# First token tiles as half-depth transposes, weights on ScalarE's queue, and partial accumulation groups at the start of a two-branch attention kernel

## The chip, the cores and the metric

The kernel runs on one core of a Trainium2 chip. The metric is device time in microseconds of that core: the median of the fast runs. A profile of one execution is there for every kernel. "Start of the K projection" below is the start of the first matmul of the second stage in such a trace; it measures the first stage, the only one that the change touches. In the profiles PE is TensorE (PEld its weight loads), DVE VectorE, ACT ScalarE, POOL GpSimd and SP the sync engine; the granted clock is the share of TensorE's full clock that the throttle let through.

## The reference

```python
def reference(A_x, A_wqkv, A_wo, B_x, B_wqkv, B_wo, gate_w):   # x: 1 x 2048 x 1024, bf16
    x = A_x
    g = sigmoid((x * gate_w).sum(-1, keepdims=True))
    a = linear_attention(x, A_wqkv, A_wo)        # 32 heads of 32, phi = elu + 1
    b = dilated_local_attention(x, B_wqkv, B_wo) # window 8, dilation 2, softmax
    return g * a + (1 - g) * b
```

The kernel first computes branch B's values, V = x @ wqkv[:, 2048:3072], for 16 token tiles of 128, in two halves of 512 columns each; then K and Q, attention and the rest.

## The kernel before

`xT` holds x transposed: 8 blocks of 128 model dimensions ("depth") on the partitions, tokens along the free axis. A DMA transpose fills it, one token tile per instruction. `ws[0]` holds the 1024 value columns as two halves; half 0 comes in four pieces of two depth blocks (256 KB each). SP is the engine that issues most DMAs, and it does so in order; the rest of its stream is stores of V.

```python
def load_x(t, prio):                      # a full tile: 128 tokens x 1024, 256 KB
    e_, r = t // 8, t % 8
    P.op("sp", lambda e: e.dma_start_transpose(xT[:, :, t*128:(t+1)*128], x2[e_, r*128:(r+1)*128, :]), ...)
def load_w(slot, half, src, c0, prio, d0=0, d1=8, eng="sp", after=()):
    P.op(eng, lambda e: e.dma_start(ws[slot][:, d0:d1, half*512:half*512+512], src[:, d0:d1, c0:c0+512]), ...)

load_x(0, 0)
load_w(0, 0, Bw, 2048, 0.1, 0, 2, "act")
load_w(0, 0, Bw, 2048, 0.2, 2, 4, "act")
load_w(0, 0, Bw, 2048, 0.3, 4, 6)
load_w(0, 0, Bw, 2048, 0.4, 6, 8)
for t in range(1, NT): load_x(t, 3 + t)
for d in range(0, 8, 2): load_w(0, 1, Bw, 2560, 6.1 + 0.1 * d, d, d + 2)   # second weight half
# ... 9 warm-up matmuls on a zero tile go ahead of everything on PE ...
for t, half in [(4*b + i, half) for b in range(NT // 4) for half in range(2) for i in range(4)]:
    # ...
    step = 2 if t == 0 else 8
    for d in range(0, 8, step):
        o = group(bank, xs, w, [xr, ws[0].part((d, d + step), ...)], d, d + step)   # 8 matmuls 128x128x512
    move(vt[:, :], bank.ap, 512, bank, vt.all())       # eviction on ScalarE or VectorE
    P.op("sp", ... store of vt to HBM ..., prio=5)
```

A planner orders each engine's instructions from estimated costs and priorities (a low number goes first). A changed cost or priority can therefore also reorder stages that the edit does not touch.

## Time and profile before

495.04 us (three runs, 494.76 to 495.15).

The page of the kernel before: its span, the busy time of each engine, and the group of V-type matmuls (count, busy time, mean ns, idle time ahead of them).

```profile
span 493.6 us, 11394 instructions
...
PE 477.7 (97%) x5055; PEld 226.2 (46%) x5121; DVE 274.7 (56%) x487; ACT 166.9 (34%) x287; POOL 5.1 (1%) x27
...
L1313 PE MATMUL ps_all<-w,xT 128*128 128x512 bf16 x921 | 207.5, 380 | 5.4 <-issue 4.3
...
```

TensorE is busy for 97% of the span. There are 5121 weight loads but only 5055 matmuls, and 921 in a group that has 960 in the changed kernel's page. So 66 matmul records are missing, and where one is, the trace seems to show a gap. I fell for this in the prediction: the "gaps of about 0.16 us per attention fill", and the "stall" of 0.22 us at 15.4 us, are missing records. The latter recurs after every 49 records (at 26.19 us again, the starts 0.431 us apart, two matmuls' time), and traces with all records have neither.

Stretches of 5 us of the kernel before: busy time (number of instructions) for each engine, granted clock, mean busy share of the DMA engines (the packets' times over that of 16 engines, so it can exceed 1), and what they moved.

```profile
...
core 0: us, PE busy (x) PEld busy (x) DVE busy (x) ACT busy (x) POOL busy (x), PEclk, DMA share, GB/s
...
5.00:10.00 5.00, 4.63 (x19) 1.74 (x19) 0.43 (x2) 0.64 (x2) 0.61 (x3) 1.00 1.10 253
10.00:15.00 5.00, 4.93 (x24) 2.05 (x23) 0.69 (x1) 1.15 (x2) 0.00 (x0) 1.00 1.07 263
15.00:20.00 5.00, 4.95 (x24) 2.29 (x24) 0.69 (x1) 1.19 (x2) 0.00 (x0) 1.00 0.87 208
...
```

The DMA issues of SP in the first 11 us of the kernel before: start, duration, what, count.

```profile
...
0.80 1.37 SPq L1287 DMA_TRANSPOSE xT<-in_A_x_dram  x1
2.23 1.07 SPq L1292 DMA_DIRECT2D w<-in_B_wqkv_dram  x2
3.35 4.82 SPq L1287 DMA_TRANSPOSE xT<-in_A_x_dram  x3
8.21 2.13 SPq L1292 DMA_DIRECT2D w<-in_B_wqkv_dram  x4
...
```

Reading: a full transpose occupies SP for about 1.3 us (one of the three at 3.35 us took 2.18, presumably with the queue full) and a plain weight piece for about 0.5. The second weight half goes out at 8.2 us, when four tiles are on their way.

The waits of PE and of its weight loads (PEld) from 5 to 30 us, before: who waited for what, total us, times, longest.

```profile
...
PEld ps_all L1313 <- DMA xT<-in_A_x_dram: 1.8, 2, 1.3
...
PEld ps_all L1313 <- DMA w<-in_B_wqkv_dram: 0.8, 2, 0.6
...
PE ps_all L1313 <- DMA xT<-in_A_x_dram: 0.4, 1, 0.4
```

One short wait for the first tile, one for the second at 8.0 us, one for the second weight half at 14.7 us.

### The profile page before, as it was taken

What the parts mean: (1) busy time and instruction counts of PE and PEld (TensorE: products, weight loads), DVE (VectorE), ACT (ScalarE), POOL (GpSimd) and SP (SyncE); (2) the same over time, 40 slices, a digit from 0 to 9 for tenths busy, and PEclk for the clock granted to TensorE, in tenths of its full rate; (3) what the DMA queues carried; (4) which work ended last, traced back from release to release, by engine and by line L of the source; (5) the groups of instructions that cost most, each with busy time, mean ns of one, the idle gap of its engine ahead of it and who ended that gap; (6) DMA issues with size and microseconds to landing.
All of it is one profiled execution on the core that took longest, in us unless ns stands there. A gap on an engine that the chain in (4) does not pass through costs nothing.

```text
span 493.6 us, 11394 instructions
## 1 busy us (share of the span) xinstructions
PE 477.7 (97%) x5055; PEld 226.2 (46%) x5121; DVE 274.7 (56%) x487; ACT 166.9 (34%) x287; POOL 5.1 (1%) x27
## 2 busy tenths in 40 slices
PE   8999999999999999999999999999999999999995
PEld 3444444444444445545554544444444444444442
DVE  2112345899676785564555555596865735524443
ACT  2111111222334345656565465455432223020000
POOL 3000000000000000000000000000000000000000
PEclk9999999999999999999999999999999999999999
DMA  8989992222003155111010100503564325101122
GB/s 225 212 206 322 307 371 62 86 86 85 14 23 110 29 161 141 28 36 35 24 35 25 35 3 3 171 1 80 124 182 117 76 38 153 65 1 66 65 85 68
DMA packets 51067, 48.80 MB, mean 99 GB/s; under 512 B 20161, under 2 KB 38977, under 8 KB 51010
## 3 DMA queue, kind: packets, MB, share of 16 engines
q1 hardware_dynamic: 50466, 47.47, 34.5%
q8 instruction: 42, 0.69, 0.6%
q10 hardware_dynamic: 544, 0.52, 0.3%
q14 instruction: 15, 0.12, 0.1%
HBM read 34.34 MB, written 9.44 MB: 89 GB/s over the span
## 4 chain that ended last, share of the span: by engine, by line
PE 89%; DMA 3%; SPq 3%; issue 2%; DVE 2%; ACT 1%; ACTq 0%
PE ps_all L1313 71%; PE ps_all L1634 11%; PE ps_all L1405 2%; PE ps_all L1424 2%; DMA rb<-rc_hbm 1%; SPq L1287 1%; PE ps_all L1506 1%; SPq L1598 1%; DMA w<-in_B_wqkv_dram 1%; PE ps_all L1431 1%; DMA rc_hbm<-ra 1%; DVE zsel L1548 1%; SPq L1292 1%; DVE pq L1326 0%; PE ps_all L1585 0%
## 5 line engine op out<-in xcount | busy, mean ns | idle before, releaser
L1313 PE MATMUL ps_all<-w,xT 128*128 128x512 bf16 x921 | 207.5, 380 | 5.4 <-issue 4.3
L1313 PE MATMUL ps_all<-xT,w 128*128 128x512 bf16 x748 | 167.5, 379 | 2.3 <-issue 1.7
L1313 PEld LDWEIGHTS ps_all<-w,xT 128*128 128x128 bf16 x960 | 91.3, 98 | 109.8 <-DMA xT<-in_A_x_dram 1.8
L1313 PEld LDWEIGHTS ps_all<-xT,w 128*128 128x128 bf16 x768 | 73.7, 98 | 89.1 <-issue 1.8
L1634 PE MATMUL ps_all<-w,qT 128*128 128x512 bf16 (+1 forms) x259 | 55.3, 373 | 0.3
L1634 PEld LDWEIGHTS ps_all<-w,qT 128*128 128x128 bf16 x264 | 25.8, 98 | 29.7
L1324 DVE TENSOR_SCALAR e<-e 128x512 bf16<-128x512 bf16 x64 | 18.3, 291 | 33.8 <-ACT e L1320 17.2
L1344 DVE CAST vst<-ps_all 128x512 bf16<-128x512 f32 x15 | 10.4, 692 | 44.0 <-PE ps_all L1313 44.0
L1411 ACT ACTIVATE E<-ps_all 128x1824 bf16<-128x1824 f32 (+1 forms) x18 | 30.4, 1687 | 9.8 <-PE ps_all L1405 9.0
L1322 ACT ACTIVATE e<-ps_all 128x512 bf16<-128x512 f32 x32 | 19.1, 597 | 42.8 <-PE ps_all L1313 42.8
L1414 DVE TENSOR_TENSOR E<-E,msk 128x1824 bf16<-128x1824 bf16 (+1 forms) x18 | 19.8, 1102 | 22.1 <-ACT E L1411 22.1
L1638 DVE SCALAR_TENSOR_TENSOR o<-ps_all,gm,xT 128x512 bf16<-128x512 f32 (+1 forms) x25 | 18.2, 730 | 23.0 <-PE ps_all L1634 22.8
L1320 ACT ACTIVATE e<-ps_all 128x512 bf16<-128x512 f32 x32 | 19.1, 597 | 26.8 <-PE ps_all L1313 25.8
L1345 ACT ACTIVATE vst<-ps_all 128x512 bf16<-128x512 f32 x17 | 10.1, 597 | 47.7 <-PE ps_all L1313 47.7
L1274 DVE TENSOR_TENSOR mx<-mx,kT 128x1024 bf16<-128x1024 bf16 x32 | 20.8, 688 | 9.3 <-ACT kT L1345 9.2
L1274 DVE TENSOR_TENSOR mx<-mx,qT 128x1024 bf16<-128x1024 bf16 x32 | 20.8, 687 | 6.9 <-ACT qT L1348 6.7
L1443 DVE TENSOR_TENSOR qT<-ps_all,L 128x456 bf16<-128x456 f32 (+1 forms) x36 | 21.0, 627 | 6.2 <-ACT L L1441 5.0
L1326 DVE SCALAR_TENSOR_TENSOR pk<-ps_all,e 128x512 bf16<-128x512 f32 x32 | 21.9, 688 | 0.7
L1440 ACT ACTIVATE L<-ps_all 128x456 f32<-128x456 f32 (+1 forms) x36 | 17.8, 547 | 12.4 <-PE ps_all L1424 12.4
L1345 ACT ACTIVATE kT<-ps_all 128x512 bf16<-128x512 f32 x16 | 9.6, 597 | 35.8 <-PE ps_all L1313 35.8
L1601 DVE TENSOR_TENSOR xT<-xT,rb 128x512 bf16<-128x512 bf16 x24 | 16.3, 689 | 8.7 <-DMA rb<-rc_hbm 8.5
L1348 ACT ACTIVATE qT<-ps_all 128x512 bf16<-128x512 f32 x16 | 9.6, 597 | 31.5 <-PE ps_all L1313 31.5
(72 smaller groups left out, 284.1 us busy)
## 6 DMA issues: line engine op xcount, KB each, us to landing
rb<-rc_hbm SPq DMA_DIRECT2D x32, 256.0 KB, 5.1
w<-in_A_wqkv_dram SPq DMA_DIRECT2D x6, 1024.0 KB, 8.5
v<-vB_hbm SPq DMA_DIRECT2D x36, 128.0 KB, 2.9
vB_hbm<-vst SPq DMA_DIRECT2D x32, 128.0 KB, 5.9
w<-in_B_wqkv_dram SPq DMA_DIRECT2D x4, 1024.0 KB, 9.0
xn<-in_A_x_dram SPq DMA_DIRECT2D x16, 256.0 KB, 2.7
out_dram<-o SPq DMA_DIRECT2D x15, 256.0 KB, 2.0
w<-in_A_wo_dram SPq DMA_DIRECT2D x8, 256.0 KB, 4.1
```

Source lines behind the costliest of these rows:

```text
L1274: P.op("dve", lambda e, m=m, op=op: e.tensor_tensor(m[:, 0:n], m[:, 0:n], src, op), 0.08 + n / 1920.0, reads=[m.all(), reg], writes=[m.all()],
L1313: last = e.matmul(bank.ap(), lhs(dc), rhs(dc), start=(dc == 0), stop=(dc == 7))
L1320: P.op("act", lambda e: e.activation(e_[:, :], bank.ap(), ACT.Exp), act(512), reads=[bank.iv], writes=[e_.all()])
L1322: P.op("act", lambda e: e.activation(e_[:, :], bank.ap(), ACT.Exp, accum_out=qe[:, col:col + 1]), act(512) + 0.1, reads=[bank.iv], writes= ...
L1324: P.op("dve", lambda e: e.tensor_scalar(e_[:, :], e_[:, :], 1.0, 1e-6, op0=ALU.min, op1=ALU.add), 0.25, reads=[e_.all()], writes=[e_.all()])
L1326: P.op("dve", lambda e: e.scalar_tensor_tensor(out=dst, in0=bank.ap(), scalar=0.0, in1=e_[:, :], op0=ALU.max, op1=ALU.add), dps(512), read ...
L1345: fa = lambda e: e.activation(dst, src(), ACT.Copy)
L1411: P.op("act", lambda e: e.activation(E[:, 0:32 * nq].rearrange("p (j q) -> p j q", j=4), ps[:, 4:8, 0:8 * nq], ACT.Exp), act(32 * nq), rea ...
L1414: P.op("dve", lambda e: e.tensor_tensor(ev(), ev(), m[:, :, :].rearrange("p r q -> p (r q)")[:, None, :].to_broadcast([128, 16, 2 * nq]), ...
L1443: P.op("dve", lambda e, L=L, h=h, q0=q0: e.tensor_tensor(qT[:, :, q0:q0 + nq], SO[h].ap(0, n).rearrange("p (c q) -> p c q", c=8), L[:, 0:n ...
L1634: last = e.matmul(bank.ap(0, f1 - f0), qT[:, dc, t * 128:(t + 1) * 128], ws[3][:, dc, f0:f1], start=(dc == 0), stop=(dc == 7))
L1638: P.op("dve", lambda e, bank=bank, o_=o_, t=t, n=n, i0=i0, i1=i1, tgt=tgt, c0=c0: e.scalar_tensor_tensor(out=o_[:, i0 * 128:i1 * 128].rear ...
```

## The change

The intent: let the first matmuls start on half of a tile's depth and half of the weights, take weight issues off SP, and delay the need for the second weight half by running eight token tiles, not four, on the first. The first pass does depth blocks 0 to 3 of tiles 0 to 3 into four PSUM banks, the second pass blocks 4 to 7.

```diff
-        load_x(0, 0)
-        load_w(0, 0, Bw, 2048, 0.1, 0, 2, "act")
-        load_w(0, 0, Bw, 2048, 0.2, 2, 4, "act")
-        load_w(0, 0, Bw, 2048, 0.3, 4, 6)
-        load_w(0, 0, Bw, 2048, 0.4, 6, 8)
-        for t in range(1, NT):
-            load_x(t, 3 + t)
         for d in range(0, 8, 2):
-            load_w(0, 1, Bw, 2560, 6.1 + 0.1 * d, d, d + 2)
+            load_w(0, 0, Bw, 2048, 0.1 + 0.1 * d, d, d + 2, "act")
+        for b in range(2):
+            for t in range(4):
+                P.op("sp", lambda e, t=t, b=b: e.dma_start_transpose(xT[:, 4 * b:4 * b + 4, t * 128:(t + 1) * 128], x2[0, t * 128:(t + 1) * 128, 512 * b:512 * b + 512]),
+                     0.8, writes=[xT.part((4 * b, 4 * b + 4), (t * 128, (t + 1) * 128))], prio=4 * b + t, chan="x%d_%d" % (t, b), lat=0.6)
+        for t in range(4, NT):
+            load_x(t, 8 + t)
...
-        for t, half in [(4 * b + i, half) for b in range(NT // 4) for half in range(2) for i in range(4)]:
+        for t, half in [(t, half) for t0, n in ((0, 8), (8, 4), (12, 4)) for half in range(2) for t in range(t0, t0 + n)]:
...
-            bank = main.next()
...
-            step = 2 if t == 0 else 8
-            for d in range(0, 8, step):
-                o = group(bank, xs, w, [xr, ws[0].part((d, d + step), (half * 512, half * 512 + 512))], d, d + step)
+            cuts = [0, 8]
+            if t < 4 and half == 0:
+                cuts = [0, 2, 4, 6, 8] if t == 0 else [0, 4, 8]
+                if t == 0:
+                    first = [main.next() for _ in range(4)]
+                    for t_ in range(4):
+                        for d, d1 in ((0, 2), (2, 4)) if t_ == 0 else ((0, 4),):
+                            group(first[t_], x_tile(t_)[0], w, [...], d, d1)
+                    o = P.ops[-1]
+                    for d in range(0, 8, 2):
+                        load_w(0, 1, Bw, 2560, 3 + 0.1 * d, d, d + 2, "act", after=[o])
+                cuts = cuts[len(cuts) // 2:]
+                bank = first[t]
+            else:
+                bank = main.next()
+            for d, d1 in zip(cuts, cuts[1:]):
+                o = group(bank, xs, w, [...], d, d1)
```

More of the change, by code (lines that the diff above doesn't have):

```diff
@@ L1356, in plan @@
                  (12, 1): (3, 0, Aw, 1024, 25), (14, 1): (3, 1, Aw, 1536, 26)}
-        for t, half in [(4 * b + i, half) for b in range(NT // 4) for half in range(2) for i in range(4)]:
+        for t, half in [(t, half) for t0, n in ((0, 8), (8, 4), (12, 4)) for half in range(2) for t in range(t0, t0 + n)]:
             vt, vs = vst.next()
             xs, xr = x_tile(t)
-            bank = main.next()
             w, wr = w_half(0, half)
-            step = 2 if t == 0 else 8
-            for d in range(0, 8, step):
-                o = group(bank, xs, w, [xr, ws[0].part((d, d + step), (half * 512, half * 512 + 512))], d, d + step)
+            cuts = [0, 8]
[5 more added lines that the diff above has]
+                        for d, d1 in ((0, 2), (2, 4)) if t_ == 0 else ((0, 4),):
+                            group(first[t_], x_tile(t_)[0], w, [xT.part((d, d1), (t_ * 128, t_ * 128 + 128)), ws[0].part((d, d1), (0, 512))], d, d1)
+                    o = P.ops[-1]
[6 more added lines that the diff above has]
+            for d, d1 in zip(cuts, cuts[1:]):
+                o = group(bank, xs, w, [xT.part((d, d1), (t * 128, t * 128 + 128)), ws[0].part((d, d1), (half * 512, half * 512 + 512))], d, d1)
             move(vt[:, :], bank.ap, 512, bank, vt.all())
```

## The prediction

> **What bounds the kernel.** TensorE. The page gives PE 477.7 us busy of 493.6 (97%), with the granted clock full in the 40 slices. Busy time by windows is 89.6 of 90 us from 20 to 110 us; later there are gaps of about 0.16 us per attention fill and one of 1 us near 370 us. Only start-up losses can be won.
>
> **Start-up losses, from the start times in the trace.** Nine warm-up matmuls run from 1.25 to 5.27 us. The first real matmul starts at 5.62, released by the first token tile (landed at 5.58). The first real matmuls start 0.40, 0.43 and 0.31 us apart, later ones 0.216: the clock rises at about 6.7 us. This agrees with the Trainium skill, "TensorE: Matmul & The Clock Gate", Part 1 (cold array at half rate, full after a few us of activity). Then come stalls: about 0.19 us at 8.0 (second token tile, landed 7.97), 0.24 at 14.7 and 0.22 at 15.4 us (second weight half; the waits view names the same DMAs). Sum: 0.35 late start, 0.48 slow clock, 0.64 stalls. The change does not move the clock, and the warm-ups stay ahead on PE: the first real matmul cannot start before 5.27. As those 0.35 us lie in the slow clock, starting earlier wins only half of them. So at most 0.18 + 0.64 = 0.8 us is to be had.
>
> **What it moves.** Matmuls, weight loads and evictions stay in number and shape. Four full transposes (about 1.3 us of SP issue each) become eight halves; I estimate 0.7 to 0.8 us each. ScalarE issues the four first-half weight pieces (0.45 us each) from 0.8 to 2.7 us, SP only transposes. The second weight half is issued by ScalarE after the first 16 matmuls instead of by SP at 8.2 us. Data need for PE: before, 3 MB (both weight halves, 4 tiles) for 64 matmuls; after, 3 MB too (one weight half, 8 tiles), but tile 4 is needed after 32.
>
> **Will data keep up?** DMA moves about 290 GB/s in this stage (windows). The Trainium skill, "DMA: Bandwidth & Descriptors", Queues, rings and completion order, says that each DMA engine round-robins between queues per packet; the trace agrees: from 4.0 to 4.5 us 143 packets of 256 B (transpose) beside 120 of 1024 B (ScalarE's queue). So weights get most bandwidth: 1 MB of weights by about 6.4 us, with the first halves of tiles 0 and 1 beside them. Estimated landings of half tiles: 4.2, 6.7 (needed 6.9), 7.4 (7.8), the others 8 to 10 (from 9.5). Tiles 4 to 7 about 11, 12, 15.5, 16.5 (needed 13, 14.6, 16.4, 18). Just in time; I expect a new stall of 0 to 0.4 us.
>
> **Prediction.** Gain 0.18 + 0.64 - 0.15 = about 0.65 us: 494.4 us, range 493.0 to 495.9. Faster by over 2%: 0.005, within 2%: 0.985, slower: 0.01.
>
> **Signs.** First real matmul at 5.3 us, not 5.6; no wait for weights at 14 to 16 us; half transposes of 0.65 to 0.85 us on SP; the 128th real matmul about 0.65 us earlier; slices from 20 us on unchanged, PE busy about 477. Wrong if: half transposes cost as much issue as full ones, so that tiles 4 to 7 come late and stalls appear at 12 to 18 us; ScalarE blocks on its DMA issues and evictions hold banks; or the re-made instruction order shifts a later stage (rb reads near 370 us, tail) by a microsecond.

## More of the kernel before

The transposes up to 30 us: count, min/median/max ns that they occupy SP, and time from issue to landing.

```profile
...
L1287 SPq DMA_TRANSPOSE xT<-in_A_x_dram x13: 1248/1308/2569, 0.8 to 28.9; - x13
...
DMA to landing us min/median/max: 3.2/4.1/5.3
```

## The result

| | median us | runs | ratio, 95% interval |
|---|---|---|---|
| before | 495.1 | 6 (494.76 to 496.3) | |
| changed | 501.99 | 6 (499.54 to 503.08) | 1.0130 (1.0105 to 1.0156) |

A ratio is the mean time of one kernel's fast runs over that of the other's of the same rounds, so it is not quite the ratio of the medians. The change made the kernel slower by 1.3%, where a gain of 0.13% had been forecast.

The page of the changed kernel, profiled in its fastest run (499.54 us), so it shows 4 of the 6.9 us between the medians:

```profile
span 497.7 us, 11467 instructions
...
PE 484.9 (97%) x5121; PEld 226.2 (45%) x5121; DVE 274.1 (55%) x484; ACT 168.7 (34%) x290; POOL 5.1 (1%) x27
...
L1312 PE MATMUL ps_all<-w,xT 128*128 128x512 bf16 x960 | 213.9, 379 | 5.9 <-DMA xT<-in_A_x_dram 5.9
...
```

The stretches of 5 us, as for the kernel before:

```profile
...
5.00:10.00 5.00, 2.52 (x11) 0.91 (x11) 0.43 (x2) 0.00 (x0) 0.62 (x3) 1.00 1.17 214
10.00:15.00 5.00, 5.00 (x24) 2.05 (x21) 2.08 (x3) 0.00 (x0) 0.00 (x0) 1.00 0.61 138
15.00:20.00 5.00, 1.90 (x9) 0.70 (x8) 0.69 (x1) 0.60 (x1) 0.00 (x0) 1.00 1.21 243
...
```

From 5 to 10 us PE is busy 2.52 us instead of 4.63, and from 15 to 20 us 1.90 instead of 4.95. From 10 to 15 us the DMA engines move 138 GB/s where they moved 263.

What PE did in the first 30 us of the changed kernel (start, length, what, count, idle time ahead and what ended it):

```profile
...
6.04 1.04 PE L1312 MATMUL ps_all<-w,xT 128*128 128x512 bf16 x4 [0.77 <-DMA xT<-in_A_x_dram]
8.79 6.22 PE L1312 MATMUL ps_all<-w,xT 128*128 128x512 bf16 x28 [1.70 <-DMA xT<-in_A_x_dram]
16.27 1.90 PE L1312 MATMUL ps_all<-w,xT 128*128 128x512 bf16 x8 [1.27 <-DMA xT<-in_A_x_dram]
20.30 9.89 PE L1312 MATMUL ps_all<-w,xT 128*128 128x512 bf16 x45 [2.13 <-DMA xT<-in_A_x_dram]
```

Four gaps, 5.87 us in all, each ended by a token tile. The waits of the same stretch agree, and no other wait has taken their place:

```profile
...
PEld ps_all L1312 <- DMA xT<-in_A_x_dram: 8.5, 5, 2.6
PE ps_all L1312 <- DMA xT<-in_A_x_dram: 5.9, 4, 2.1
...
```

SP's issues:

```profile
...
0.80 10.51 SPq L1299 DMA_TRANSPOSE xT<-in_A_x_dram  x8
11.35 9.17 SPq L1287 DMA_TRANSPOSE xT<-in_A_x_dram  x4
20.56 0.58 SPq L1378 DMA_DIRECT2D vB_hbm<-vst  x1
...
```

Eight halves occupy SP until 11.3 us. Tile 4 is issued at 11.35 us; before, all four tiles and both weight halves were out at 10.3. The transposes by line (the first line is the halves), and the landings up to 30 us:

```profile
...
L1299 SPq DMA_TRANSPOSE xT<-in_A_x_dram x8: 1245/1270/1330, 0.8 to 10.0; - x8
L1287 SPq DMA_TRANSPOSE xT<-in_A_x_dram x8: 1247/1310/3812, 11.3 to 29.4; - x8
...
DMA to landing us min/median/max: 2.7/4.4/7.8
```

The half transposes take 1.27 us of SP each, the full ones 1.31.

The budget from the two traces: the first real matmul starts 0.42 us later (6.04 against 5.62), the V stage from there to the K projection takes 60.88 us instead of 56.18, and the rest is 1.1 us shorter (425.12 against 426.23 us from the start of the K projection to PE's end). Together +4.0 us. The 1.1 us belong to no part of the change: e6_order below has before's instruction order on PE and 425.12 us too, and over all profiles of these kernels the rest takes 425.12 to 426.23 us. It is mostly one gap of 0.98 us at 370 us in the one trace of before. With a single trace of that kernel I can't tell how often it has it.

### The profile page after: what moved, and what is told of

Its sections match the earlier page's. It is cut to its first block, busy times and chain, and to the rows that moved or that the text cites. A ratio compares the mean times of both kernels' runs of the same rounds, so it can differ in the third digit from the quotient of the medians.

```text
span 497.7 us, 11467 instructions
## 1 busy us (share of the span) xinstructions
PE 484.9 (97%) x5121; PEld 226.2 (45%) x5121; DVE 274.1 (55%) x484; ACT 168.7 (34%) x290; POOL 5.1 (1%) x27
## 3 DMA queue, kind: packets, MB, share of 16 engines
HBM read 34.34 MB, written 9.44 MB: 88 GB/s over the span
## 4 chain that ended last, share of the span: by engine, by line
PE 93%; SPq 2%; DMA 2%; DVE 1%; issue 0%
PE ps_all L1312 76%; PE ps_all L1646 11%; PE ps_all L1417 2%; SPq L1299 2%; PE ps_all L1436 2%; DMA xT<-in_A_x_dram 2%; PE ps_all L1518 1%; PE ps_all L1443 1%; DVE zsel L1560 1%; PE ps_all L1597 0%; DVE pq L1325 0%; SPq L1287 0%; PE ps_all L1570 0%; DVE e L1323 0%; DVE w L1343 0%
## 5 line engine op out<-in xcount | busy, mean ns | idle before, releaser
L1312 PE MATMUL ps_all<-w,xT 128*128 128x512 bf16 x960 | 213.9, 379 | 5.9 <-DMA xT<-in_A_x_dram 5.9
L1312 PE MATMUL ps_all<-xT,w 128*128 128x512 bf16 x768 | 170.7, 379 | 0.0
L1426 DVE TENSOR_TENSOR E<-E,msk 128x1824 bf16<-128x1824 bf16 (+1 forms) x18 | 19.8, 1102 | 22.1 <-ACT E L1423 22.1
L1344 ACT ACTIVATE kT<-ps_all 128x512 bf16<-128x512 f32 x18 | 10.7, 597 | 34.7 <-PE ps_all L1312 34.7
L1325 DVE SCALAR_TENSOR_TENSOR pk<-ps_all,e 128x512 bf16<-128x512 f32 x32 | 21.9, 687 | 0.7
L1347 ACT ACTIVATE qT<-ps_all 128x512 bf16<-128x512 f32 x18 | 10.8, 597 | 31.1 <-PE ps_all L1312 31.1
```

Of the source, the lines that this page charges most:

```text
L1312: last = e.matmul(bank.ap(), lhs(dc), rhs(dc), start=(dc == 0), stop=(dc == 7))
L1325: P.op("dve", lambda e: e.scalar_tensor_tensor(out=dst, in0=bank.ap(), scalar=0.0, in1=e_[:, :], op0=ALU.max, op1=ALU.add), dps(512), read ...
L1344: fa = lambda e: e.activation(dst, src(), ACT.Copy)
L1426: P.op("dve", lambda e: e.tensor_tensor(ev(), ev(), m[:, :, :].rearrange("p r q -> p (r q)")[:, None, :].to_broadcast([128, 16, 2 * nq]), ...
```

## The experiments

Two theories. The **issue theory**: a DMA transpose occupies SP for about 1.27 us whatever its depth, so halving tiles 0 to 3 costs four extra instructions and halves the rate at which tokens arrive. The **share theory**: weight pieces on ScalarE's queue reach the DMA engines ahead of the transposes on SP's, which land late. Third suspects: the order of eight tiles, the partial groups, the second weight half on ScalarE's queue, and the clock.

All runs gave correct results; ratios are to the kernel before in the same rounds. "First" and "K" are the start of the first real matmul and of the K projection in the one profiled run.

| run | what | median us | ratio (95%) | first | K |
|---|---|---|---|---|---|
| before | | 494.9 to 495.7 | 1 | 5.62 | 61.80 |
| changed | | 501.99 | 1.0130 (1.0105 to 1.0156) | 6.04 | 66.93 |
| after_again | the same, again | 501.70 | 1.0123 (1.0109 to 1.0138) | 5.33 | 69.34 |
| e1_full | changed, halves undone | 502.21 | 1.0138 (1.0108 to 1.0168) | 6.14 | 67.77 |
| e2_w1late | changed, second weight half on SP | 500.81 | 1.0101 (1.0086 to 1.0115) | 5.94 | 70.90 |
| e3_w_back | changed, two first-half pieces back on SP | 501.35 | 1.0135 (1.0117 to 1.0153) | 5.46 | 67.83 |
| e4_halves_only | before, halves alone | 499.46 | 1.0091 (1.0078 to 1.0104) | 5.66 | 65.89 |
| e5_act_weights_only | before, two pieces to ScalarE alone | 497.20 | 1.0049 (1.0033 to 1.0066) | 6.13 | 63.27 |
| e6_order | before, order of eight alone | 495.91 | 1.0005 (0.9991 to 1.0019) | 5.70 | 63.16 |
| e9_partial_order | before, order and partial groups | 497.33 | 1.0043 (1.0026 to 1.0060) | 5.77 | 63.62 |
| e10_halves_order | before, order and halves | 500.65 | 1.0110 (1.0093 to 1.0127) | 5.62 | 67.39 |
| e8_fill | changed, stalls filled | 501.27 | 1.0127 (1.0112 to 1.0141) | 5.50 | 68.21 |
| e12_full_fill | e1_full, stall filled | 499.96 | 1.0080 (1.0061 to 1.0099) | 6.05 | 66.74 |
| e7_order_den | e6, denominators later | 495.51 | 0.9995 (0.9981 to 1.0009) | 5.80 | 63.32 |
| e11_order_w1soon | e6, second half sooner | 495.27 | 1.0000 (0.9987 to 1.0013) | 5.86 | 62.32 |

### e0_sizes: what a transpose costs SP

```diff
-        for t in range(1, NT): load_x(t, 3 + t)
+        for t in [1, 2, 3, 4, 5, 6, 7, 13, 15]: load_x(t, 3 + t)
+        # tile 8: 4 x (128 rows x 256 columns), tile 9: 8 x (128 x 128), tile 10: 2 x (64 x 1024),
+        # tile 11: 2 x (128 x 512), tile 12: 4 x (32 x 1024), tile 14: 8 x (16 x 1024)
```

> The kernel before, with tiles 8 to 12 and 14 loaded in pieces of several shapes, to measure what one transpose costs SP. Issue theory (a transpose costs SP's queue about 1.27 us whatever its depth): pieces of 512, 256 and 128 columns by 128 rows all take 1.2 to 1.3 us where nothing blocks the queue; pieces with fewer rows tell whether rows set it. Share theory (the 1.27 us of the halves is back-pressure of the DMA engines, busy with weights): pieces issued later, when little else moves, take about 0.65, 0.35 and 0.2 us for 512, 256 and 128 columns. The kernel as a whole will be slower than before (some 25 more transposes on SP), which is of no interest.

All transposes of that run, pieces first (min/median/max ns on SP):

```profile
...
L1302 SPq DMA_TRANSPOSE xT<-in_A_x_dram x28: 1099/1176/2131, 20.0 to 71.0; - x28
L1287 SPq DMA_TRANSPOSE xT<-in_A_x_dram x10: 1237/1310/2461, 0.8 to 72.3; - x10
...
```

By shape, from the start and length of each instruction in the trace, with the queue not blocked:

| rows x columns | KB | us on SP |
|---|---|---|
| 128 x 1024 | 256 | 1.24 to 1.38 |
| 128 x 512 | 128 | 1.27 |
| 64 x 1024 | 128 | 1.27 |
| 128 x 256 | 64 | 1.17 |
| 32 x 1024 | 64 | 1.18 |
| 128 x 128 | 32 | 1.10 to 1.23 |
| 16 x 1024 | 32 | 1.10 to 1.23 |

The cost is nearly all fixed: an eighth of the bytes takes 1.10 to 1.23 us where the whole takes 1.24 to 1.38, even at 30 to 70 us, far from the crowded start. Back-pressure is ruled out as the cause of the 1.27 us, and the issue theory's premise holds. It is the cost where nothing blocks; four transposes of this run, left out of the table, took 1.58 to 2.46 us. The whole run took 516.14 us, a single look.

### after_again: the changed kernel a second time

> The changed kernel unaltered, to have it on the same chip and a second profile. Expected: ratio to before 1.010 to 1.016, first real matmul near 6.0 us, stalls of about 1.7 us near 7, 1.3 near 15 and 2.1 near 18 us. Its runs should spread by 3 us, the slower ones with a lower mean granted clock (0.991 to 0.998); if the profile catches such a run it should show matmuls 0.427 us apart for some microseconds after one of the stalls.

Ratio and stalls as expected in kind, though of other sizes: 1.50 us ahead of tile 1, 3.15 ahead of tile 4, 0.66 ahead of tile 5. This profile (502.43 us) caught what the first did not. Its stretches from 10 to 25 us:

```profile
...
10.00:15.00 5.00, 4.60 (x22) 1.86 (x19) 2.08 (x3) 0.37 (x1) 0.00 (x0) 1.00 0.79 156
15.00:20.00 5.00, 2.25 (x6) 0.88 (x7) 0.00 (x0) 0.23 (x1) 0.00 (x0) 0.66 1.21 200
20.00:25.00 5.00, 4.34 (x15) 1.44 (x14) 0.69 (x1) 0.35 (x1) 0.00 (x0) 0.65 1.08 196
...
```

The granted clock (third column from the right) falls to 0.66: from 16.65 us, within the long stall, to 23.48 us the array is at half speed, and the trace has matmuls 0.427 us apart. The clock is not all: tile 5 landed at 21.96 us here and at 20.25 in the first profile, 1.7 of the 2.4 us by which the K projection starts later. Such drops come in some runs: over the first six runs of the changed kernel the mean granted clock goes from 1.000 at a span of 497.7 us to 0.991 at 501.2. The Trainium skill, "TensorE: Matmul & The Clock Gate", Part 1, describes the like: an array that was idle falls back to half clock. How idle it was here is in the last section.

### e1_full: halves undone

```diff
-        for b in range(2):
-            for t in range(4):
-                P.op("sp", ... half transpose ...)
+        for t in range(4):
+            load_x(t, t)
```

> The changed kernel with tiles 0 to 3 loaded by four full transposes, all else kept (weights on ScalarE's queue, order of eight tiles, partial groups). Issue theory: tiles 4 to 7 are issued at about 6.0, 7.3, 8.6, 9.9 us instead of 11.3 to 16.7, all stalls after the first matmul vanish or stay under 0.5 us; the time falls by 5 us or more against the changed kernel, to 494 to 496. Share theory (weight packets of ScalarE's queue pass ahead of the transposes): tile 1 still lands at 8.5 to 9 us, a stall of 1.5 to 2.5 us stays near 7 us, only the later ones go; 496 to 498.

PE in this run:

```profile
...
6.14 1.04 PE L1310 MATMUL ps_all<-w,xT 128*128 128x512 bf16 x4 [0.94 <-DMA xT<-in_A_x_dram]
9.97 15.70 PE L1310 MATMUL ps_all<-w,xT 128*128 128x512 bf16 x60 [2.80 <-DMA xT<-in_A_x_dram]
26.32 4.06 PE L1310 MATMUL ps_all<-w,xT 128*128 128x512 bf16 x18 [0.64 <-DMA w<-in_B_wqkv_dram]
```

The time did not move (502.21 us), which neither theory's number foresaw. The share theory is right on the first stall: tile 1, a full one, lands at 9.93 us, 7.7 us after its issue. No gap follows at tiles 4 to 7, as both theories said. But tile 4 was issued at 9.56 us, not at the 6.0 of the issue theory: the full transposes of tiles 2 and 3 occupied SP for 3.30 and 2.51 us, so 1.3 us is the cost of a full one only where nothing blocks it, and undoing the halves brought tile 4's issue forward by 1.8 us only. Yet 60 matmuls from 9.97 us take 15.7 us where 13.1 would do at full clock, so something else ate the gain; e12_full_fill follows it up.

### e2_w1late: second weight half moved to SP

```diff
-                    for d in range(0, 8, 2):
-                        load_w(0, 1, Bw, 2560, 3 + 0.1 * d, d, d + 2, "act", after=[o])
+        for d in range(0, 8, 2):                      # behind tile 7
+            load_w(0, 1, Bw, 2560, 15.1 + 0.1 * d, d, d + 2)
```

> The changed kernel with only the second weight half moved: from ScalarE's queue (after 16 matmuls) to SP's, behind tile 7. Halves stay. Share theory: tile 5 lands about 3.5 us after its issue at 12.7, not 7.5; the stalls near 15 and 18 us (3.4 us together) shrink to under 1 us in all, that near 7 us stays at 1.7; about 3 us faster than the changed kernel. Issue theory: tile 4 is still issued at 11.3 us, so the stalls near 15 and 18 us stay above 2 us together; within 1.5 us of the changed kernel.

```profile
...
8.69 14.59 PE L1314 MATMUL ps_all<-w,xT 128*128 128x512 bf16 x60 [1.71 <-DMA xT<-in_A_x_dram]
26.84 13.36 PE L1314 MATMUL ps_all<-w,xT 128*128 128x512 bf16 x49 [3.56 <-DMA w<-in_B_wqkv_dram]
```

(PE again.) The two stalls ahead of tiles 4 and 5 are gone: tile 5, issued at 12.68 us, lands at 17.07, after 4.4 us instead of 7.5. So the second weight half on ScalarE's queue did hold the tiles up. (In part the stalls are hidden: the clock was at half from 8.27 to 11.69 us, so PE came to tile 4 some 1.5 us late. At full clock, I estimate from the start times, about 0.8 us of stall would be left ahead of tile 4 and none ahead of tile 5.) The expected 3 us did not come, only about 1: the weight half, now issued between 17.5 and 21.5 us, was late itself and cost 3.56 us in this run (504.02 us, the slowest of five), with a second stretch of half clock after it (25.34 to 32.17 us).

### e3_w_back: two pieces back on SP

```diff
-        for d in range(0, 8, 2):
+        for d in range(0, 4, 2):
             load_w(0, 0, Bw, 2048, 0.1 + 0.1 * d, d, d + 2, "act")
+        for d in range(4, 8, 2):                      # between the first and the second halves of the tiles
+            load_w(0, 0, Bw, 2048, 3.1 + 0.1 * d, d, d + 2)
```

> The changed kernel with weight pieces three and four of the first half back on SP's queue, between the halves of tile 3 and the second half of tile 0; halves and order of eight tiles kept. Share theory: with two pieces on ScalarE's queue, not four, the first half of tile 1 lands by 6.5 us instead of 8.3 to 8.7; the stall of 1.5 to 1.7 us near 7 us falls under 0.6 us; the first 16 matmuls are done by 9.7 us, not 11.0 to 11.4. Issue theory: SP still has eight halves and now two more issues ahead of tile 4, which is issued at 12.4 us, so the stalls near 15 and 20 us stay, 3 us or more together. Both true: 498 to 501 us, faster than the changed kernel by about 1 us or equal.

```profile
...
5.46 3.79 PE L1314 MATMUL ps_all<-w,xT 128*128 128x512 bf16 x16 [0.18 <-DMA xT<-in_A_x_dram]
11.02 1.04 PE L1314 MATMUL ps_all<-w,xT 128*128 128x512 bf16 x4 [1.77 <-DMA xT<-in_A_x_dram]
12.80 1.89 PE L1314 MATMUL ps_all<-w,xT 128*128 128x512 bf16 x4 [0.74 <-DMA xT<-in_A_x_dram]
16.07 14.15 PE L1314 MATMUL ps_all<-w,xT 128*128 128x512 bf16 x56 [1.38 <-DMA xT<-in_A_x_dram]
```

(PE.) Both theories are borne out, though the time (501.35 us) is just above the 498 to 501 I gave. The stall near 7 us is gone: the half tile that landed at 8.74 us now lands at 5.64, though SP issues it at the same 2.18 us. Then stalls of 1.77, 0.74 and 1.38 us, all for second halves of token tiles, which SP issues from 7.23 us. The third is not of issue alone: that half landed 6.24 us after its issue, beside the second weight half on ScalarE's queue. The gaps sum to 4.07 us, less than the changed kernel's 5.87, but the clock was at half from 12.67 to 19.49 us, and the time is that of the changed kernel. Landing times of the transposes issued in the first 6 us, in the changed kernel and then in this one:

```profile
...
DMA to landing us min/median/max: 4.6/5.3/6.6
```

```profile
...
DMA to landing us min/median/max: 2.7/3.1/4.5
```

### e4_halves_only: halves alone in the kernel before

```diff
-        load_x(0, 0)
+        for b in range(2):
+            for t in range(4):
+                P.op("sp", ... half transpose ..., prio=(0 if t == 0 else 3 + t) + 0.05 * b)
...
-        for t in range(1, NT): load_x(t, 3 + t)
+        for t in range(4, NT): load_x(t, 3 + t)
```

> The kernel before with only the transposes of tiles 0 to 3 halved (both halves of a tile after one another), weights and order as before. Issue theory: each tile takes 2.6 us of SP instead of 1.3, so the first matmul starts near 6.5 us, tile 3 and the second weight half go out 4 to 5 us later than before, PE stalls for 2 to 4 us up to the 64th real matmul, and perhaps a drop of the clock on top: 497 to 500 us. Share theory alone: halves cost nothing, 495 to 496 us.

499.46 us: halves alone cost 0.9%, some 4.5 us. Tile 3 is whole at 13.75 us (before: 10.13), and the second weight half is issued from 12.39 us (before: 8.21). The first matmul still starts at 5.66 us, earlier than I had expected.

### e5_act_weights_only: the two pieces alone in the kernel before

```diff
-        load_w(0, 0, Bw, 2048, 0.3, 4, 6)
-        load_w(0, 0, Bw, 2048, 0.4, 6, 8)
+        load_w(0, 0, Bw, 2048, 0.3, 4, 6, "act")
+        load_w(0, 0, Bw, 2048, 0.4, 6, 8, "act")
```

> The kernel before with only the third and fourth piece of the first weight half moved to ScalarE's queue; full transposes and order as before. Share theory: tile 1, though issued a microsecond earlier than before, lands at 9 to 10 us instead of 8.0, and the fourth weight piece at 8 to 10 us instead of 7.2; PE stalls 2 to 4 us before 12 us, with a drop of the clock on top in most runs: 498 to 502 us. Issue theory alone: SP gains a microsecond, 494.5 to 495.5 us.

Transposes issued in the first 6 us, before and then in this run:

```profile
...
DMA to landing us min/median/max: 4.4/4.6/4.8
```

```profile
...
DMA to landing us min/median/max: 5.2/6.8/7.2
```

The same bytes are to be moved, but transposes now take 6.8 us to land, not 4.6. Tile 1, issued 1.1 us earlier, lands 1.5 us later (9.44 against 7.97 us). The fourth weight piece, issued at 2.28 us, lands at 9.26; on SP, issued at 2.85, it had landed at 7.18. So the move delayed both kinds of load. The cost is 0.5%, 2.3 us, below the range I gave (498 to 502 us), and with no visible drop of the clock (means of 0.997 to 0.999, as the kernel before).

### e6_order, e9_partial_order and e10_halves_order: order and partial groups

```diff
# e6_order, against before: the order of eight tiles, and
-            load_w(0, 1, Bw, 2560, 6.1 + 0.1 * d, d, d + 2)
+            load_w(0, 1, Bw, 2560, 10.1 + 0.1 * d, d, d + 2)     # behind tile 7
# e9_partial_order: the changed kernel with this loading (halves and both moves of weights undone)
# e10_halves_order: e6_order with the halves of e4_halves_only
```

> The kernel before with only the order changed: eight tiles with the first weight half, then eight with the second, and the second weight half issued by SP behind tile 7. Full transposes and first-half weights as before. If the order itself is harmless and the loss is halves plus ScalarE's weights: the waits for weights near 14.7 and 15.4 us are gone, tiles 4 to 7 land before they are needed (full transposes bring 256 KB per 1.3 us, a tile is used up in 1.73 us), the K projection starts at 61.3 to 61.5 us instead of 61.8, 494.3 to 494.8 us. If the order is a cause of its own: stalls at tiles 4 to 7, K projection at 63 us or later, 496.5 us or more.

> The changed kernel with halves and both moves of weights undone together: full transposes, first-half weights as before, second half on SP behind tile 7; the partial groups and the order of eight tiles stay. Undoing one alone won nothing (three runs), so either each alone is enough to hold PE up, and then this one is back at 494.3 to 496 us with the K projection starting before 63 us; or what all of them kept (partial groups, order) is the cause, and it stays at 499 us or more. A stall of up to 1 us may remain, as the partial groups want tiles 1 to 3 earlier (all four first passes within 4 us).

> The kernel before with halves (both of a tile one after another) and the order of eight tiles, second weight half on SP behind tile 7, no extra weights on ScalarE's queue. Issue theory in numbers: a half brings 128 KB per 1.31 us of SP, 100 GB/s, and the order uses tokens up at 256 KB per 1.73 us, 152 GB/s; so PE stalls along the halves and tiles 4 to 7: the K projection starts at 64 to 66 us, 2 to 4 us later than before, time 497 to 499.5. If halves hurt only beside weights on ScalarE's queue: 495 to 496.

The waits of PE from 5 to 30 us, in e9_partial_order (first line) and in e10_halves_order:

```profile
...
PE ps_all L1313 <- DMA w<-in_B_wqkv_dram: 1.9, 1, 1.9
...
```

```profile
...
PE ps_all L1316 <- DMA xT<-in_A_x_dram: 3.1, 4, 0.9
PE ps_all L1316 <- DMA w<-in_B_wqkv_dram: 2.6, 5, 0.9
...
```

The order alone is level with before (1.0005), a miss of my expected gain. In its trace the V stage is 1.3 us longer (57.47 against 56.18 us), and the rest 1.1 us shorter. It loses no time at tiles 4 to 7, but about 1.5 us at the second weight half, whose pieces were issued between stores (15.4 to 18.4 us) and landed from 18.7 to 23.0. With the partial groups too the ratio is 1.0043, above the range I gave; its profile has one long gap, 1.86 us, again for that late weight half. e9 and e6 ran in the same rounds and their code differs in the groups alone, so the groups, with whatever they shift, cost about 1.4 us (497.33 against 495.91). Why is not shown: the two profiles differ by 0.9 us, 0.4 of it in the V stage. Undoing halves and weights together thus brings the changed kernel from 501.7 to 497.3 us, though not all the way back. Undoing the halves alone won nothing (e1); of the weights, undoing one move at a time won about 1 us (e2) or nothing (e3), and both moves undone with halves and groups kept was not run. And halves with the order, without extra weights on ScalarE's queue, give 1.0110, nearly all of the loss and more than I had expected (500.65 us against 497 to 499.5): the issue theory needs no help from the queue. Its stalls go to token tiles and weights in about equal parts, as both wait in SP's stream.

### e8_fill and e12_full_fill: the clock

```diff
+        def idle(n):       # n matmuls on the zero tile, into the warm-up bank
+            ...
# e8_fill: changed kernel, idle(7) after the first four real matmuls, idle(5) and idle(9) ahead of tiles 4 and 5
# e12_full_fill: e1_full, idle(12) after the first four real matmuls
```

> The changed kernel with 21 idle matmuls on the warm-up tile (7, 5 and 9 of 0.216 us, less than the stalls measured) put where it stalls: after the first four real matmuls and ahead of tiles 4 and 5. If part of the loss, and its spread between runs, is the clock that falls to half after long stalls, these runs show no matmuls 0.427 us apart after the start, mean granted clock of 0.998 or more, a spread under 1.5 us, and 498.5 to 500 us, 2 us faster than the changed kernel although more work was added. If the stalls alone set the time: as the changed kernel, 501 to 502.5.

> e1_full with 12 idle matmuls on the warm-up tile in its first stall (2.8 us, before tile 1). If the half clock from 8.4 to 15.2 us explains why undoing the halves alone won nothing: with the array kept busy no matmuls 0.427 us apart after 8 us, the first 16 real matmuls done by 13 us instead of 15.1, the K projection about 2 us earlier than 67.8, the time 499 to 500.5 us (e1_full 502.2), ratio 1.008 to 1.011. If the clock does not matter (as e8_fill suggests): within 0.7 us of e1_full, ratio 1.012 to 1.016.

In e8_fill the mean clock is back at 0.997 or more and the spread shrinks to 1 us, but the median stays (501.27 us). My expectation failed: there, it seems, the slow clock runs mostly while PE waits anyway (tile 5 landed at 21.5 us in this run, 22.0 in after_again), so it costs little. In e1_full the data is there when the clock is low, and filling the stall wins 2.2 us between the medians; the ratios' intervals do not overlap, but the two profiled runs happen to differ by 0.2 us only (501.09 and 500.89). The stretches from 5 to 15 us of e1_full, then of e12_full_fill:

```profile
...
5.00:10.00 5.00, 1.26 (x6) 0.34 (x6) 0.43 (x2) 0.00 (x0) 0.63 (x3) 0.84 1.22 214
10.00:15.00 5.00, 5.00 (x12) 1.76 (x13) 0.00 (x0) 0.60 (x1) 0.00 (x0) 0.50 1.15 192
...
```

```profile
...
5.00:10.00 5.00, 4.23 (x11) 1.41 (x11) 0.43 (x2) 0.00 (x0) 0.61 (x3) 1.00 1.21 203
10.00:15.00 5.00, 5.00 (x25) 2.28 (x24) 0.69 (x1) 0.60 (x1) 0.00 (x0) 1.00 1.17 199
...
```

PE is busy all of 10 to 15 us in both, but at clock 0.50 does 12 matmuls and at 1.00 it does 25. So undoing the halves did help; a stall of 2.8 us and the half clock after it hid that. With the stalls filled in both, undoing the halves takes the ratio from 1.0127 (e8) to 1.0080 (e12).

### e7_order_den and e11_order_w1soon: a version that beats both?

```diff
# e7: e6_order and
-                after(3, lambda u=u: over(u))
+                after(4, lambda u=u: over(u))
# e11: e6_order with the second weight half issued once tile 2's first group is done
+            if (t, half) == (2, 0):
+                for d in range(0, 8, 2):
+                    load_w(0, 1, Bw, 2560, 4 + 0.1 * d, d, d + 2, after=[o])
```

> Attempt at a version that beats both: e6_order and, apart from the change, the denominator matmuls of a chunk issued one group later, as the plan of the changed kernel had it by chance. Expected: gain of e6_order (0.3 to 0.5 us) plus the 1.0 us gap that PE has before the third denominator group in the kernel before: 493.2 to 494 us. Rest of the program after the start of the K projection 425.1 to 425.3 us instead of 426.2.

> e6_order again, with the second weight half issued by SP earlier: ahead of the stores, as soon as the third tile's first group is done, about 12 to 14 us instead of 15.4 to 18.4. If the 1.5 us that e6_order still lost near 22 us was only this late issue, the four pieces land by 19 us, no PE gap over 0.3 us is left after 9 us, the K projection starts at 61.4 to 61.8 us (before 61.8, e6_order 63.2), and the time is 494 to 495 us, ratio to before 0.997 to 1.000. If the order of eight tiles itself asks for too much data at once: a stall of 1 us or more at tiles 4 to 7 or at the second half, K projection at 62.5 us or later.

Neither is shown to be faster: 0.9995 and 1.0000. e7's rest of the program takes 425.12 us, as e6_order's, so moving the denominators did nothing. (The expectation's premise was wrong too: from the K projection on, the changed kernel's trace has the denominators where the kernel before has them.) e11 issued the weights at 14.9 to 16.9 us only, since SP got to them late; they landed by 22.1 and stalls of about 0.6 us were left. Its V stage takes 56.46 us against 56.18. The kernel before remains the best.

## Why the prediction was wrong

- **The room for a gain was about right.** 0.8 us was to be had by my sum; 0.22 of it was a missing record. A ceiling of 0.6 us was right reason to expect nothing much.
- **The step that failed: "Four full transposes (about 1.3 us of SP issue each) become eight halves; I estimate 0.7 to 0.8 us each."** Measured 1.27 us. Only one size was in the trace, and I took the cost to fall nearly with the bytes. e0_sizes shows that it is nearly fixed. With 1.31 us per issue the prediction's own sums change sign: tile 4 goes out at 0.8 + 8 x 1.31 = 11.3 us, and as no transpose of the profile before landed in under 3.2 us, not before 14.5, where I had it needed at 13. In rates: 128 KB per 1.31 us is 100 GB/s, while the order of eight tiles uses 256 KB per 1.73 us, 152 GB/s. The prediction named this as a way to be wrong, but gave it no weight in the range.
- **"Tiles 4 to 7 about 11, 12, 15.5, 16.5" and "a new stall of 0 to 0.4 us" failed with it.** They landed at 16.2, 20.3, 21.9 and 22.7 us, and PE lost 6.4 us instead of 0.35 + 0.42 before, both by start times as in the prediction (5.87 us of it as gaps of the timeline).
- **The share of the queues, and the rate, were mis-sized.** I counted 143 transpose packets beside 120 of ScalarE's in half a microsecond and took packets one for one. From 3.5 to 5.5 us of the changed kernel it was 78 beside 454 (but 579 beside 335 with the full transposes of e1, so no fixed share), and the first half of tile 1 landed at 8.74 us, not 6.7. The weights were late too: the fourth piece landed at 8.38 us, not 6.4. From 2 to 8.4 us the DMA engines moved 232 GB/s, where the kernel before moved 287 and I had reckoned with 290. Two more pieces on ScalarE's queue cost 2.3 us alone (e5), without any new bytes, and the second weight half there held tiles 4 and 5 up (e2). Whether the DMA engines' turns or the making of descriptors held the transposes back is not settled by these runs.
- **The clock after a stall was not considered.** "The change does not move the clock" holds in the first profile but not in most runs. It is worth about 2.2 us once the halves are undone (e12), but in the changed kernel itself filling the stalls did not lower the median (e8).
- **Right:** the order of eight tiles by itself costs no time (e6), though its V stage grew by 1.3 us, and later stages keep their length but for 1.1 us.

Put into the kernel before, halves cost 4.5 us and two pieces on ScalarE's queue 2.3; the changed kernel lost 6.1 to 6.9. That the two sum to about as much is no proof that they add: order and groups cost 1.7 more by themselves (e9), and the second weight half moved as well. What tells is that each suffices to starve PE, so undoing one leaves the other (e1, e3), and that undoing both does help, by about 4 us (e9).

## What to carry to other kernels

Before cutting a DMA into smaller ones, measure what one issue costs at both sizes; with only one size in the trace, carry the fixed-cost case through the sums as well and let the range cover it. Compare supply with use as rates in the order of need (here 100 against 152 GB/s), and remember that moving loads to a second queue changes who lands first even if the bytes are the same. When a single undo wins nothing, undo in pairs before dropping the suspect, and look at the granted clock before blaming the data.

## What the Trainium skill lacked or had wrong

- "DMA: Bandwidth & Descriptors", DMA Transpose (X-bar): constraints, but no cost of issue. (Elsewhere the page has one count of sequencer cycles for small transposes of "previous generations", not by size.) The runs show 1.10 to 1.38 us of the issuing engine for 32 to 256 KB where nothing blocks it, against 0.42 to 0.58 us for a plain 256 KB piece in the kernel before.
- The same page, Issuing engines are not separate DMA queues, says that issuing from several engines only saves the sequencer's issue time. Two pieces moved from SP to ScalarE cost 2.3 us (e5_act_weights_only), since transposes then took 6.8 us to land instead of 4.6. That section has no warning that the order of landing changes.
- "TensorE: Matmul & The Clock Gate", HAM oscillation: "The abstract rule is 'no PE-idle gaps >~3.4µs.'" The runs show falls without any such gap (in e3_w_back none was over 1.77 us). In the traces the clock changes on a grid of 3.413 us, and what tells falls from none is PE's busy share of the last 3.41 us on that grid: 40% or less before all seven falls in the 16 traces (those after the last matmuls left out), 43% or more in every stretch without one. So in e2_w1late gaps of 0.81 and 1.71 us, four matmuls between them, sufficed (busy 1.31 us from 4.86 to 8.27), while in the first profile of the changed kernel 0.77 and 1.70 us did not (1.58 us from 5.92 to 9.33). This is read from these traces alone, and no run was made to test it.
- No page that I read says that matmul records can be missing so regularly: 66 of 5121, one after every 49 in the first stage, which look like gaps of 0.05 to 0.2 us or stalls.
